# Loading v straight behind k and q in a pooled-attention and gated-feed-forward kernel, with the fourth batch's k and q loaded inside the pooling of the third batch's v

## The chip, the cores and the metric

The kernel runs on one core of one Trainium2 chip. The metric is the device time of one execution in microseconds (us). Several unprofiled executions give a median. One further execution was recorded by the hardware profiler, and every instruction time below comes from that one. In the profile PE is TensorE (PEld its weight load), DVE is VectorE, ACT is ScalarE, POOL is GpSimd, and SP is the engine whose queue issues most of the hardware DMAs.

## What is computed

There are 8 batches (numbered 0 to 7 in the code; "the third batch" is number 2, "the fourth" number 3), 8 heads, 576 positions and a head width of 64. The reference, cut to what matters:

```
k_p, v_p = k, v averaged over groups of 8 positions      # 72 keys and values per head
attn = softmax(q @ k_p.T / 8)                            # 576 x 72 per head
x    = (attn @ v_p) as a matrix of 4608 tokens x 512
h    = x @ w_in                                          # 512 -> 2048
out  = (h * cos(h)) @ w_out                              # 2048 -> 512, float32
```

## The kernel before

The feed-forward part works in nine token tiles of 512, `t` = 0 to 8. A batch is 576 tokens, so tile `t` ends inside batch `t`; its last 64 tokens of batch `t-1` (`REST`) and most of batch `t` make it up. The order of every engine is written out by hand: each engine executes its instructions in program order, and between engines only semaphores hold an instruction back.

Stage `t` of the main loop (L448) first runs the up projection on PE (`up_mm`, L320; 8 pairs of column groups, `fp`), while ACT takes the cosine (L327) and DVE multiplies (L330). It then runs the down projection on PE (`down_mm`, L333; 64 matmuls, counted by `n`). Between these 64 matmuls stand, at places given by the list `fill` (L508), the attention of batch `b = t+1`: scores (L213), exponentials (L220), and `values_rows`, which multiplies with the pooled values (L300), normalises on DVE (L301, L303) and sends the result `x_r` through a DMA transpose on SP's queue into `xT` (L304). There are four such transposes in a stage, a first pair (`n` = 18 and 19) and a second pair (`n` = 42 and 44). `xT` is what the next stage's up projection reads. For stage 2 (tile columns 1024 to 1535) that includes the first three of the four transposed blocks of batch 2; every later stage needs fewer blocks of its newest batch.

The inputs of attention are staged by POOL, and these are what the change touches:

- `load_kv` (L100 to L105) issues a DMA on POOL's own queue that reads k or v of a batch in float32 and leaves bf16. Its tile comes from a pool of two buffers (`kvst`) that k and v take in turn, so v(b) uses the buffer that v(b-1) used, and k(b) that of k(b-1). `load_q` (L107) does the same for q, whose tiles have two buffers of their own.
- `pool_add` (L134) adds up the groups of 8 on POOL: one large add (L141), one half its output's size (L144), then for k two small ones into `kp2` (L147) and for v one into `vz` (L150). Its argument `then` is called after the first add.
- `q_transpose` (L186) and `k_transpose` (L173) are DMA transposes on SP's queue, issued in the up projection of stage `t` after `fp` 0 and `fp` 2. They make `qT` and `kk`, which the scores read.
- The copy into `gate` (L525) is a one-element copy that reads `kk`. It makes POOL wait until the k transpose has landed before it issues the next batch's loads.

At the end of stage `t`'s code stand POOL's steps for batch `b+1`, so POOL's order for it is: gate, load k, load q, first add of k, load v, rest of k, all of v:

```
        if 0 < t and b + 1 < B:

            nc.gpsimd.tensor_copy(out=gate, in_=kk[b % 2][0:1, 0, 0:1])
        if b + 1 < B:
            load_kv(b + 1, "k", k)
            load_q(b + 1)
            pool_add(b + 1, "k", lambda: load_kv(b + 1, "v", v))
            pool_add(b + 1, "v")
```

Batches 0 and 1 are loaded and pooled differently (on PE) and the change leaves them alone.

Of the kernel before, what the change touches and what calls it, by code (L numbers as in the profile page):

```python
# [12 lines left out]
ADD = mybir.AluOpType.add  # L13
# [6 lines left out]
def kernel(  # L20
# [9 lines left out]
    nc = tc.nc  # L30
    B, H, S, D = q.shape
# [35 lines left out]
    kk = [wpool.tile([128, H, SpA], BF16, name=f"kk{i}") for i in range(2)]  # L67
# [10 lines left out]
    staged = {}  # L78
# [4 lines left out]
    def load_even(dst, b, src, j0=0, j1=KCH):  # L83
        nc.gpsimd.dma_start(out=dst[:, j0:j1].rearrange("p j t d -> p j (t d)"), in_=even_view(src, b, j0, j1))  # L84

    def kv_tile():
        return kvst.tile([128, 2 * H * POOL * D], BF16, name="kv_st", tag="kv_st")
# [9 lines left out]
    def q_tile(b):  # L97
        staged["q", b] = qst.tile([128, KCH, ROW, D], BF16, name="q_b", tag="q_b")

    def load_kv(b, which, src):  # L100

        st = kv_tile()[:Sp].rearrange("p (i h t d) -> p i h t d", i=2, h=H, t=POOL)
        nc.gpsimd.dma_start(out=st[:, 0].rearrange("p h t d -> p h (t d)"),
                            in_=src[b].rearrange("h (p t) d -> p h (t d)", t=POOL))
        staged[which, b] = st  # L105

    def load_q(b):  # L107
        q_tile(b)
        load_even(staged["q", b], b, q)
# [15 lines left out]
    def v_part(b):  # L125
        return vz[b % 2][:, :, 0:4:3, :]
# [4 lines left out]
            for r in range(2):  # L131
                copy(out=dst[half[r], pj0:pj1, a, 0:Sp], in_=ps[half[a]])

    def pool_add(b, which, then=None):  # L134

        st = staged.pop((which, b))
        x = st[:, 0]
        s = st[:, 1].rearrange("p h t d -> p (h t d)").bitcast(FP32).rearrange(
            "p (h t d) -> p h t d", h=H, t=POOL // 2)
        add = nc.gpsimd.tensor_tensor  # L140
        add(out=s, in0=x[:, :, 0:4, :], in1=x[:, :, 4:8, :], op=ADD)  # L141
        if then is not None:
            then()
        add(out=s[:, :, 0:2, :], in0=s[:, :, 0:2, :], in1=s[:, :, 2:4, :], op=ADD)  # L144
        if which == "k":
            for slot in range(2):
                add(out=kp2[b % 2][:Sp, :, slot, :], in0=s[:, :, 0, :], in1=s[:, :, 1, :], op=ADD)  # L147
        else:
            s = s.rearrange("p (j a) t d -> p j a t d", a=2)
            add(out=v_part(b), in0=s[..., 0, :], in1=s[..., 1, :], op=ADD)  # L150

    def pool_k_mm(b, bank, pj0, pj1):

        kb = staged["k", b]
        ps = bank[:, 0:(pj1 - pj0) * Sp].rearrange("p (j n) -> p j n", n=Sp)
        for pj in range(pj0, pj1):
            for t in range(ROW):
                for rows in half:
                    nc.tensor.matmul(ps[rows, pj - pj0, :], lhsT=kb[rows, pj, t, :], rhs=groups[rows, t, :],  # L159
                                     start=(t == 0), stop=(t == ROW - 1))  # L160
        return lambda copy: put_kk(b, ps, pj0, pj1, copy)
# [10 lines left out]
    def k_transpose(b):  # L172
        nc.sync.dma_start_transpose(out=kk[b % 2], in_=kp2[b % 2].rearrange("p h s d -> p (h s d)"))  # L173
# [14 lines left out]
    def q_transpose_mm(b, bank, g0, g1):  # L188

        if ("qT", b) not in att:  # L190
            qT_tile(b)
        ps = bank.bitcast(BF16)[:, 0:(g1 - g0) * 128].rearrange("p (g n) -> p g n", n=128)
        for g in range(g0, g1):
            nc.tensor.matmul(ps[:, g - g0, :], q_flat(b)[:, g * 128:(g + 1) * 128], identity, is_transpose=True)  # L194
        return lambda copy: copy(out=att["qT", b][:, g0:g1, :], in_=ps)
# [114 lines left out]
    def sin_tables():  # L310
        nc.scalar.preload_act_table_set("trig_and_small")  # L311


    def up_mm(t, fp, k0=0, k1=KCH):

        h = banks[fp % 3]
        for j in range(2):
            fc = 2 * fp + j
            for ki in range(k0, k1):
                nc.tensor.matmul(h[:, j, :], lhsT=w_in_sb[fc // 4][:, ki, (fc % 4) * 128:(fc % 4 + 1) * 128],  # L320
                                 rhs=xT[:, ki, t * TILE:(t + 1) * TILE],
                                 start=(ki == 0), stop=(ki == KCH - 1))

    def up_g(t, fp, between=()):
        h = banks[fp % 3]
        cos = msb.tile([128, 2, TILE], FP32, name="cos", tag="cos", bufs=2)
        nc.scalar.activation(out=cos, in_=h, func=ACTF.Sin, bias=half_pi[:, :1])  # L327
        for put, copy in between:
            put(copy)
        nc.vector.tensor_mul(out=g_sb[:, 2 * fp:2 * fp + 2, :], in0=h, in1=cos)  # L330
# [38 lines left out]
    for rows in half:  # L369
# [15 lines left out]
                            in1=first_of.unsqueeze(1).to_broadcast([128, ROW, Sp]), op=mybir.AluOpType.subtract)  # L385
# [6 lines left out]
    gate = consts.tile([1, 1], BF16, name="gate")  # L392
# [52 lines left out]
    up_mm(0, 1, 0, 2)  # L445
    sin_tables()

    for t in range(NT):  # L448
        b = t + 1
        if t > 0:  # L450

            up_mm(t, 0, 0, 2)
            up_mm(t, 1, 0, 2)
        for fp in range(FFCH // 2):
            up_mm(t, fp, 2 if fp < 2 else 0)
            between = ()
            if t == 0:
                if fp == 4:
                    puts = pool_k_mm(1, obanks[0], 0, 2), pool_k_mm(1, obanks[1], 2, 4)
                elif fp in (5, 6):  # L460
                    g0 = 9 * (fp - 5)
                    puts = q_transpose_mm(1, obanks[0], g0, g0 + 5), q_transpose_mm(1, obanks[1], g0 + 5, g0 + 9)
                if fp in (4, 5, 6):
                    puts[0](vec)
                    between = ((puts[1], act),)
            up_g(t, fp, between)
            if 0 < t and b < B:
                if fp == 0:
                    q_transpose(b)
                elif fp == 2:  # L470
                    k_transpose(b)
        mms = [(ms, fc) for ms in range(4) for fc in range(FFCH)]
        if t == 0:
            mms = [(ms, fc) for hm in range(2) for cg in range(4) for ms in range(2 * hm, 2 * hm + 2)
                   for fc in range(4 * cg, 4 * cg + 4)]


        def S_(n, bank):
            return lambda: scores(b, us[n], banks[bank])

        later = []

        def V_(n, bank, wait=None):
            return lambda: values(b, us[n], banks[bank], wait)

        fill = []
        if t < B:
            exp_tables()
            fill = [(1, lambda: scores(t, REST, banks[2])), (16, lambda: values(t, REST, banks[1]))]
        if t == 0:  # L490
            fill[1:] = [(2, S_(0, 0)), (8, lambda: pool_v_mm(1, banks[1])), (8, lambda: values(t, REST, banks[2])),
                        (11, S_(1, 0)), (13, V_(0, 1)), (18, S_(2, 2)), (21, V_(1, 0, later)), (26, S_(3, 1)),
                        (32, lambda: later.pop()()), (32, V_(2, 2)), (40, V_(3, 0))]
        elif b < B:
            us = BY_TOKENS

            def scores_of(*parts):

                def go():
                    for f in scores_mm, scores_exp:  # L500
                        for b_, u, bank in parts:
                            f(b_, u, banks[bank])
                return go

            def rows_of(i, blk, bank):
                return lambda: values_rows(b, us[2 * i:2 * i + 2], blk, banks[bank])

            fill = [(4, scores_of((b, us[0], 2), (b, us[1], 0))), (18, rows_of(0, 0, 1)), (19, rows_of(0, 1, 2)),  # L508
                    (29, scores_of((b, us[2], 0), (b, us[3], 1), (t, REST, 2))),
                    (42, rows_of(1, 0, 0)), (44, rows_of(1, 1, 1)), (47, lambda: values(t, REST, banks[2]))]  # L510
        fi = 0
        if t == NT - 1:
            mms = mms[:-FFCH]
        for n, (ms, fc) in enumerate(mms):
            while fi < len(fill) and fill[fi][0] <= n:
                fill[fi][1]()
                fi += 1
            down_mm(obanks[ms % 2], ms, fc)
            if fc == FFCH - 1:
                down_out(t, ms, obanks[ms % 2])  # L520
        if t < B:
            sin_tables()
        if 0 < t and b + 1 < B:

            nc.gpsimd.tensor_copy(out=gate, in_=kk[b % 2][0:1, 0, 0:1])  # L525
        if b + 1 < B:
            load_kv(b + 1, "k", k)
            load_q(b + 1)
            pool_add(b + 1, "k", lambda: load_kv(b + 1, "v", v))
            pool_add(b + 1, "v")  # L530
    last_chunk()
# [1 line left out]
_INS = ['q', 'k', 'v', 'moe_w_in', 'moe_w_out']  # L533
# [26 lines left out]
```

## Time and profile before

| what | value |
|---|---|
| median of 3 unprofiled runs | 300.61 us (299.97 to 300.97) |
| the profiled execution's own time | 303.76 us |
| its span, first to last instruction | 302.0 us |
| mean granted TensorE clock | 0.988 of full |
| PE busy | 287.4 us (95% of the span) |
| DVE, ACT, POOL busy | 158.7, 162.0, 130.6 us |
| packets of POOL's DMA queue (q0) | 18.07 MB, 39.9% of 16 engines' span |
| packets of SP's DMA queue (q1) | 17.57 MB, 31.0% |

The profiled execution is 3.15 us longer than the median, and 1.76 us of its time lies around the span. A timeline line gives start, duration, engine, line of the kernel, operation, output and input, count, and in brackets how long the engine stood idle before it and what released it. A line of waits gives the engine and instruction that waited, what it waited for, the sum in us, how often, and the longest. A line of stretches gives the window, its length, the busy time of each engine with instruction counts, the granted clock as a share of full speed, the mean busy share of the 16 DMA engines (records may overlap, so it can pass 1), and GB/s. A line on a DMA's landing gives the minimum, median and maximum from issue to landing.

### The profile page before, as it was taken

What the parts mean: (1) busy time and instruction counts of PE and PEld (TensorE: products, weight loads), DVE (VectorE), ACT (ScalarE), POOL (GpSimd) and SP (SyncE); (2) the same over time, 40 slices, a digit from 0 to 9 for tenths busy, and PEclk for the clock granted to TensorE, in tenths of its full rate; (3) what the DMA queues carried; (4) which work ended last, traced back from release to release, by engine and by line L of the source; (5) the groups of instructions that cost most, each with busy time, mean ns of one, the idle gap of its engine ahead of it and who ended that gap; (6) DMA issues with size and microseconds to landing.
All of it is one profiled execution on the core that took longest, in us unless ns stands there. A gap on an engine that the chain in (4) does not pass through costs nothing.

```text
span 302.0 us, 4739 instructions
## 1 busy us (share of the span) xinstructions
PE 287.4 (95%) x1878; PEld 140.2 (46%) x1912; DVE 158.7 (53%) x212; ACT 162.0 (54%) x182; POOL 130.6 (43%) x93
## 2 busy tenths in 40 slices
PE   6889999999949999999999999999999999999995
PEld 2545544445514455445544544455445544444444
DVE  6358546574504645564557454745475547425712
ACT  3886897465504655465546554655465646605500
POOL 8463008692958296329492956284900000000000
PEclk9999999999978999999999999999999999999999
DMA  7999996929992976776998597679902430131023
GB/s 148 205 207 207 207 199 130 180 65 131 169 210 42 151 77 145 169 99 91 156 200 119 84 174 160 96 116 142 203 0 54 87 72 0 35 72 35 0 66 75
DMA packets 57221, 36.07 MB, mean 119 GB/s; under 512 B 35184, under 2 KB 52464, under 8 KB 57200
## 3 DMA queue, kind: packets, MB, share of 16 engines
q0 software_dynamic: 19744, 18.07, 39.9%
q1 hardware_dynamic: 37216, 17.57, 31.0%
q8 instruction: 15, 0.25, 0.3%
q10 hardware_dynamic: 240, 0.13, 0.2%
q14 instruction: 6, 0.05, 0.0%
HBM read 36.70 MB, written 9.44 MB: 153 GB/s over the span
## 4 chain that ended last, share of the span: by engine, by line
PE 90%; DMA 6%; issue 1%; POOL 1%; DVE 1%; DVEq 0%; POOLq 0%
PE bank L320 42%; PE obank L333 38%; DMA kv_st<-in_v_dram 3%; PE bank L213 3%; DMA xT<-x_r 3%; PE bank L300 2%; PE bank L243 1%; PE bank L351 1%; PE bank L167 1%; POOL q_b L84 1%; PE obank L159 0%; PE obank L282 0%; PE obank L194 0%; DVE xT L284 0%; DVE vz L169 0%
## 5 line engine op out<-in xcount | busy, mean ns | idle before, releaser
L320 PE MATMUL bank<-xT,w_in_sb 128*128 128x512 bf16 x564 | 128.6, 385 | 4.8 <-DMA xT<-x_r 4.2
L333 PE MATMUL obank<-w_out_sb,g_sb 128*128 128x512 bf16 x540 | 127.8, 379 | 1.3 <-issue 0.6
L327 ACT ACTIVATE cos<-bank,half_pi 128x1024 f32<-128x1024 f32 x72 | 79.2, 1113 | 77.7 <-PE bank L320 77.7
L330 DVE TENSOR_TENSOR g_sb<-bank,cos 128x1024 bf16<-128x1024 f32 x72 | 87.3, 1224 | 58.8 <-ACT cos L327 58.8
L320 PEld LDWEIGHTS <-w_in_sb 128*128 128x128 bf16 x576 | 56.6, 99 | 74.0 <-issue 4.9
L333 PEld LDWEIGHTS <-g_sb 128*128 128x128 bf16 x560 | 51.6, 98 | 56.6 <-issue 1.9
L141 POOL TENSOR_TENSOR kv_st<-kv_st 72x2048 f32<-72x2048 bf16 x12 | 48.7, 4058 | 66.7 <-DMA kv_st<-in_k_dram 46.4
L339 DVE COPY o_sb<-obank 128x512 f32<-128x512 f32 x35 | 24.2, 692 | 46.9 <-PE obank L333 45.6
L220 ACT ACTIVATE ex<-bank 72x1024 bf16<-72x1024 f32 (+1 forms) x40 | 35.0, 928 | 21.0 <-PE bank L213 20.9
L144 POOL TENSOR_TENSOR kv_st<-kv_st 72x1024 f32<-72x1024 f32 x12 | 28.3, 2355 | 0.6
L249 ACT ACTIVATE lnc<-bank 64x256 f32<-64x256 f32 (+1 forms) x24 | 10.8, 449 | 17.9 <-PE bank L243 17.7
L254 DVE TENSOR_TENSOR xT<-bank,inv 64x256 bf16<-64x256 f32 (+1 forms) x24 | 12.3, 511 | 10.8 <-ACT inv L250 10.6
L303 DVE TENSOR_TENSOR x_r<-bank,inv_r 128x512 bf16<-128x512 f32 x24 | 16.6, 692 | 0.8
L147 POOL TENSOR_TENSOR kp<-kv_st 72x512 bf16<-72x512 f32 x12 | 14.9, 1265 | 0.5
L213 PE MATMUL bank<-qT,kk 64*72 64x256 bf16 (+1 forms) x192 | 12.1, 250 | 0.3 <-issue 0.3
L308 ACT ACT_TABLE_LOAD x9 | 11.5, 1283 | 0.9 <-PEq L544 0.7
L213 PEld LDWEIGHTS <-kk 64*72 64x72 bf16 x192 | 7.9, 110 | 8.5 <-issue 7.2
L311 ACT ACT_TABLE_LOAD x9 | 11.5, 1283 | 0.2
L300 PEld LDWEIGHTS <-ex 72*128 72x128 bf16 x192 | 8.9, 97 | 5.0
L301 DVE RECIPROCAL inv_r<-bank 128x8 f32<-128x8 f32 x24 | 4.9, 203 | 10.7 <-PE bank L300 10.7
L300 PE MATMUL bank<-vz,ex 72*128 72x65 bf16 x192 | 9.8, 193 | 0.1
L84 POOL DMA_DIRECT2D q_b<-in_q_dram x10 | 7.8, 784 | 2.2 <-DMA w_in_sb<-in_moe_w_in_dram 1.4
(59 smaller groups left out, 105.1 us busy)
## 6 DMA issues: line engine op xcount, KB each, us to landing
out_dram<-o_sb SPq DMA_DIRECT2D x70, 128.0 KB, 2.9
kv_st<-in_v_dram POOLq DMA_DIRECT2D x8, 576.0 KB, 9.4
kv_st<-in_k_dram POOLq DMA_DIRECT2D x7, 576.0 KB, 7.6
q_b<-in_q_dram POOLq DMA_DIRECT2D x6, 576.0 KB, 9.6
w_in_sb<-in_moe_w_in_dram POOLq DMA_DIRECT2D x4, 512.0 KB, 13.8
w_out_sb<-in_moe_w_out_dram POOLq DMA_DIRECT2D x4, 512.0 KB, 18.2
q_b<-in_q_dram POOLq DMA_DIRECT2D x4, 288.0 KB, 12.6
g_sb<-in_k_dram SPq DMA_DIRECT2D x1, 576.0 KB, 3.6
```

The lines of the kernel that those rows point to most:

```text
L141: add(out=s, in0=x[:, :, 0:4, :], in1=x[:, :, 4:8, :], op=ADD)
L144: add(out=s[:, :, 0:2, :], in0=s[:, :, 0:2, :], in1=s[:, :, 2:4, :], op=ADD)
L147: add(out=kp2[b % 2][:Sp, :, slot, :], in0=s[:, :, 0, :], in1=s[:, :, 1, :], op=ADD)
L213: nc.tensor.matmul(pair[:Sp, bank, c:c + n].rearrange("p (g n) -> p g n", n=64), lhsT=kk[b % 2][half[r], h0 + i, 0:Sp], rhs=att["qT", b][h ...
L220: nc.scalar.activation(out=ex[:, 0:nh * n].rearrange("p (a n) -> p a n", a=2), in_=pair[:Sp, :, 0:nh * n // 2], func=ACTF.Exp, scale=scale ...
L300: nc.tensor.matmul(out[:, pj, hp * (D + 1):(hp + 1) * (D + 1)], lhsT=ex[:, c:c + 128], rhs=v1)
L303: nc.vector.tensor_mul(out=x, in0=vals, in1=inv.unsqueeze(3).to_broadcast([128, KCH, 2, D]))
L320: nc.tensor.matmul(h[:, j, :], lhsT=w_in_sb[fc // 4][:, ki, (fc % 4) * 128:(fc % 4 + 1) * 128], rhs=xT[:, ki, t * TILE:(t + 1) * TILE], st ...
L327: nc.scalar.activation(out=cos, in_=h, func=ACTF.Sin, bias=half_pi[:, :1])
L330: nc.vector.tensor_mul(out=g_sb[:, 2 * fp:2 * fp + 2, :], in0=h, in1=cos)
L333: nc.tensor.matmul(o, lhsT=g_sb[:, fc, ms * 128:(ms + 1) * 128], rhs=w_out_sb[fc // 4][:, fc % 4, :], start=(fc == 0), stop=(fc == FFCH - 1))
L339: nc.vector.tensor_copy(out=o[:, 0:n], in_=ps)
```

## The change

`pool_add` no longer calls a function between its adds. It can be run whole, or as its first add alone (`part` 0), or as all but its first add (`part` 1). The gate and the loads of k and q are put into a function `load_next`.

- In all stages the load of v is issued directly behind the load of q, before POOL's first add of k. It used to stand behind that add.
- At the end of stage 0 only the first add of v of batch 2 is issued. Its other adds come in stage 1, after `k_transpose(2)`, behind the gate and the loads of k and q of batch 3; the load of v of batch 3 follows them.
- At the end of stage 1 only the pooling adds of batch 3 are left, since its loads have been issued already.

```
@@ -131,16 +131,17 @@
-    def pool_add(b, which, then=None):
-
-        st = staged.pop((which, b))
+    def pool_add(b, which, part=None):
+
+        st = staged[which, b]
...
-        add(out=s, in0=x[:, :, 0:4, :], in1=x[:, :, 4:8, :], op=ADD)
-        if then is not None:
-            then()
+        if part != 1:
+            add(out=s, in0=x[:, :, 0:4, :], in1=x[:, :, 4:8, :], op=ADD)
+        if part == 0:
+            return
...
@@ -445,6 +446,13 @@
+    def load_next(b):
+
+        if b > 1:
+            nc.gpsimd.tensor_copy(out=gate, in_=kk[b % 2][0:1, 0, 0:1])
+        load_kv(b + 1, "k", k)
+        load_q(b + 1)
+
@@ -469,6 +477,10 @@
                 elif fp == 2:
                     k_transpose(b)
+                    if t == 1:
+                        load_next(b)
+                        pool_add(b, "v", 1)
+                        load_kv(b + 1, "v", v)
@@ -520,14 +532,12 @@
-        if 0 < t and b + 1 < B:
-
-            nc.gpsimd.tensor_copy(out=gate, in_=kk[b % 2][0:1, 0, 0:1])
         if b + 1 < B:
-            load_kv(b + 1, "k", k)
-            load_q(b + 1)
-            pool_add(b + 1, "k", lambda: load_kv(b + 1, "v", v))
-            pool_add(b + 1, "v")
+            if t != 1:
+                load_next(b)
+                load_kv(b + 1, "v", v)
+            pool_add(b + 1, "k")
+            pool_add(b + 1, "v", 0 if t == 0 else None)
```

The orders of PE, DVE, ACT and SP are the same in both kernels, instruction for instruction. POOL has the same instructions in another order.

## The prediction

> **What bounds the kernel now.** I read the span in 40 slices first. PE is at 9 tenths almost everywhere, and its clock leaves full speed in one place, slices 12 and 13 (83 to 98 us). Next came the waits, which name one large wait of PE.
>
> ```profile
> PE   6889999999949999999999999999999999999995
> PEclk9999999999978999999999999999999999999999
> ```
>
> ```profile
> PE bank L320 <- DMA xT<-x_r: 4.2, 1, 4.2
> POOL gate L525 <- DMA kk<-kp: 8.2, 2, 4.8
> ```
>
> PE's timeline puts the wait between stages 1 and 2: PE ends the down projection at 83.74 and the up projection starts at 87.94, when a transpose of x_r has landed. The chain of waits shows the same DMA on the path for 8.31 us. The stages in stretches price it:
>
> ```profile
> 79.91 3.83 PE L333 MATMUL obank<-w_out_sb,g_sb 128*128 128x512 bf16 x16
> 87.94 16.63 PE L320 MATMUL bank<-xT,w_in_sb 128*128 128x512 bf16 x63 [4.19 <-DMA xT<-x_r]
> ```
>
> ```profile
> 53.40:87.94 34.54, 30.04 (x189) 14.40 (x191) 17.41 (x23) 16.88 (x18) 22.17 (x15) 0.98 0.96 139
> 87.94:120.91 32.97, 32.80 (x189) 15.24 (x193) 16.02 (x21) 16.89 (x18) 23.81 (x13) 0.92 0.71 121
> 120.91:151.27 30.36, 30.15 (x190) 14.55 (x193) 16.71 (x22) 16.88 (x18) 15.01 (x11) 1.00 0.87 131
> 151.27:181.60 30.33, 29.91 (x189) 14.54 (x192) 16.71 (x22) 16.88 (x18) 21.23 (x12) 1.00 0.88 142
> ```
>
> Stages 3 to 6 take 30.30 to 30.40 us, PE bound. Stage 1 is longer by its wait, 4.19 us; stage 2 takes 32.97, that is 2.62 us over the mean 30.35, at a mean clock of 0.92. The wait so costs 4.19 + 2.62 = 6.81 us. Elsewhere after the start PE waits for nothing long, so this is all that POOL's order can give back.
>
> Why the transpose is late is read from landings. SP issues the second pair of stage 1 at 79.6 and 80.9, just behind v's load, which POOL issued at 78.78. It lands after 7.4 and 8.3 us. In stage 2 the second pair is issued at 116.9, v's load (from 107.48) having landed at 115.8, and it lands after 2.4 us.
>
> ```profile
> L304 SPq DMA_TRANSPOSE xT<-x_r x2: 1192/1258/1325, 79.6 to 80.9; - x2
> DMA to landing us min/median/max: 7.4/7.9/8.3
> ...
> L304 SPq DMA_TRANSPOSE xT<-x_r x2: 1191/1208/1226, 116.9 to 118.2; - x2
> DMA to landing us min/median/max: 2.4/2.4/2.4
> ```
>
> POOL's timeline gives the steps that move:
>
> ```profile
> 59.18 4.07 POOL L141 TENSOR_TENSOR kv_st<-kv_st 72x2048 f32<-72x2048 bf16 x1 [2.89 <-DMA kv_st<-in_v_dram]
> 63.33 2.35 POOL L144 TENSOR_TENSOR kv_st<-kv_st 72x1024 f32<-72x1024 f32 x1
> 65.76 1.27 POOL L150 TENSOR_TENSOR vz<-kv_st 72x512 bf16<-72x512 f32 x1
> 66.98 0.18 POOL L525 COPY gate<-kk 1x1 bf16<-1x1 bf16 x1
> 67.10 0.86 POOL L103 DMA_DIRECT2D kv_st<-in_k_dram  x1
> 67.96 0.79 POOL L84 DMA_DIRECT2D q_b<-in_q_dram  x1
> 74.76 4.06 POOL L141 TENSOR_TENSOR kv_st<-kv_st 72x2048 f32<-72x2048 bf16 x1 [6.02 <-DMA kv_st<-in_k_dram]
> 78.78 0.86 POOL L103 DMA_DIRECT2D kv_st<-in_v_dram  x1
> ```
>
> **Stage 0: v of batch 2 ahead of the first add of k.** The issue (0.87) waits for its buffer, which PE stops reading at 37.66 (pooling of batch 1's v). POOL stands idle until 46.45 for k of batch 2, so wait and issue cost nothing; k and q were issued before, and in the same queue v follows them. q landed at 28.46 + 20.7 = 49.2. v then lands by 49.2 + 8.6 = 57.8 at most (8.6 is its whole time to landing before), and by about 54 if only a load's spacing is added (k and q of one batch land 2.8 to 3.5 us apart). k's later adds start 0.87 us earlier, so k is pooled at 55.4, and v's first add runs from there, or at the latest from 57.8: it ends between 59.5 and 61.9. I take 59.5.
>
> **Stage 1: the gate and k, q of batch 3 inside v's pooling.** The gate now waits for `kk` of batch 2; queued behind it are two load issues, v's last adds, and so `vz`, which PE reads at 71.63. In this execution that k transpose was issued at 60.36 and landed 2.8 us later, 63.2. The q transpose ahead of it on SP took 4.36 us to issue beside v's load; without such a load it took 2.0 to 2.2 (stages 3, 4), so I take 58.2 for the k transpose and 61.0 for the gate; ends 61.0 and 63.2. Then k 0.86, q 0.79, adds 2.35 and 1.27, with the gaps of the listing some 5.5 us: `vz` ready at 66.5 (at most 68.7, before it was 67.03), 3 to 5 us ahead of PE. v of batch 3 is issued at 66.5, not 78.78.
>
> Its landing: at most 10.2 us (the longest v load in the rows, beside a pair of transposes) after issue, 76.7; or counted by loads, q lands 11 us after k's issue (67.10 to 78.2), 72.1, and v one load (half of the 9.4 that two need beyond 1.6 of start) later, 76.8. From the late gate 79.0. So v is in by 76.8, ahead of the second pair at 79.6. It now runs beside the first pair (73.3 and 74.7), which before ran beside q and landed after 6.1 and 7.0 us. I take those times again, 81.8 at the latest; the row for a pair that wholly runs beside v, stage 3, has 8.6 and 9.6 us, which would be 84.4. The first of the second pair, the one that PE waited for, then lands at 79.6 + 2.4 = 82.0. PE wants it at 83.74. The wait of 4.19 us goes, and with it the low clock. What is late next is the end of PE's own down projection, with about 1.7 us to spare. DVE's last write to xT ends at 82.2.
>
> The Trainium skill (TensorE: Matmul & The Clock Gate, Part 1) says an idle window of about 3.4 us halves the clock; here it was at half from 86.5 to 93.3, 2.8 us after PE stopped. By that rule any leftover wait well under 3 us would cost itself alone.
>
> A rule of the Trainium skill speaks against the change: the page DMA: Bandwidth & Descriptors (Queues, rings and completion order) has each engine take turns between queues packet by packet. My estimate by that rule is about twice 2.4 us for a pair beside v; it would land at 84.4, PE would wait 0.7 us, and there would be no more than that to win. The 7.4 to 8.3 us measured here decide against it.
>
> **Stages 2 to 6: v directly behind q.** POOL issues the same DMA one place earlier (0.86 us in an idle of 5.5 to 6.3 us for k), so k's first add is not delayed. v lands some 15 to 16 us after k's issue, not 21 to 22. In stage 3 k was issued at 128.6; v would land near 144 instead of 150.4. The first pair there is issued at 141.0 and 142.3 and landed after 8.6 to 9.6 us, near 150.8, just before the stage's end at 151.27; with v in at 144 it lands earlier. Cost 0; the cover is POOL's idle time, and without it 0.86 us per stage would fall on POOL, which has slack to the gate. I gain nothing here either, as PE waits for no DMA in these stages.
>
> **Sum.** Profiled execution: 303.76 - 4.19 - 2.62 = 296.95 us, span 295.2. The median lies 3.15 us below the profiled time. PE's stages repeat to 0.1 us, so a DMA wait is what can differ between executions, and I read the unprofiled ones as losing about 3.65 us (300.61 - 296.95) at the same place. Then they too end near 296.9. If instead recording costs all 3.15 us, 6.81 comes off 300.61: 293.8. I take 296.9, nearer the row that repeats.
>
> **Rivals.** (1) Part of the wait stays: the three loads run on into the second pair. For: three loads and a pair share 16 engines. Against: 3 us between 76.8 and 79.6. Stage 3's second pair, issued as v ended, took 4.1 to 4.8 us, which lands at 84.4 and leaves 0.7 us, 297.6; a wait of 3 us without the low clock gives 299.95.
>
> (2) The change does not do what it says: the pair was slow for its own queue (four outputs, q and k transposes follow) and not for v. Then nothing moves, 300.6. Against: the 2.4 us of stage 2 with the same SP order.
>
> (3) Slower: the gate, now in front of v's last adds, holds `vz` back. It decides when `kk` lands after 71.63 - 5.5 = 66.1; each us beyond is a us of PE wait, and from about 2.8 us another 2.6 for the clock. To end 0.9 us over the median it must land at about 69: 296.95 + 2.9 + 2.6 = 302.4. For: gate waits of 4.8 us occur. Against: in stage 1 it landed at 63.2 even beside v.
>
> **Chances.** 0.3% (0.9 us) is about what measurement tells from no change. All of the wait gone 0.72; rival 1 0.12, most of it below 299.7; rival 2 0.06; rival 3 0.10. Faster 0.72 + 0.11 = 0.83; same 0.06 + 0.01 = 0.07; slower 0.10. The range goes from 293.8 to 299.7, leaving out rivals 2 and 3 and the end of rival 1, 0.17.
>
> **What would show it.** Right: no wait of PE L320 for xT<-x_r, clock at full throughout stage 2, stages 1 and 2 both near 30.35 us; v of batch 3 issued near 66.5, gate at about 61; second pair of stage 1 landing after 2.4 us. Wrong: a PE wait at L300 in stage 1 (`vz`), or the second pair still landing after 5 us or more with v already in, or a second place that loses time where the unprofiled runs lost it.

## The result and the profile after

The changed kernel takes 296.43 us (median of 4, 296.36 to 296.98). The kernel before took 300.79 us beside it (median of 4, 299.97 to 301.95). The ratio is 0.9856, 95% interval 0.9821 to 0.9891. The profiled execution takes 296.36 us with a span of 294.6, against 303.76 and 302.0 before. The profiled execution of the kernel before was one of its slow ones, so the gain is the 4.36 us between the medians and not the 7.4 us between the profiles.

The span in 40 slices of the changed kernel has no dent in PE and no fall of its clock (line numbers are one higher than before from L141 to L446, the copy into `gate` is now L452, and the experiments shift some lines further):

```profile
PE   8899999999999999999999999999999999999995
PEclk9999999999999999999999999999999999999999
```

Its PE timeline at the end of stage 1 goes from the down projection to the up projection with no idle time in brackets. The windows of stages 1, 2 and 3 are all 30.35 or 30.36 us long, with the clock at 1.00.

```profile
79.48 3.83 PE L334 MATMUL obank<-w_out_sb,g_sb 128*128 128x512 bf16 x17
83.16 14.01 PE L321 MATMUL bank<-xT,w_in_sb 128*128 128x512 bf16 x64
```

```profile
52.80:83.16 30.36, 30.36 (x194) 14.56 (x193) 16.73 (x23) 16.89 (x18) 26.02 (x15) 1.00 0.85 138
83.16:113.51 30.35, 30.35 (x194) 14.59 (x193) 16.71 (x22) 16.89 (x18) 20.86 (x12) 1.00 0.78 136
113.51:143.86 30.35, 30.35 (x193) 14.59 (x192) 16.70 (x22) 16.89 (x18) 18.59 (x12) 1.00 0.79 136
```

The landings of stage 1's second pair of transposes, and POOL's steps that lead to it, in the changed kernel:

```profile
L305 SPq DMA_TRANSPOSE xT<-x_r x2: 1190/1214/1237, 79.1 to 80.4; - x2
DMA to landing us min/median/max: 2.5/2.5/2.5
```

```profile
61.65 0.18 POOL L452 COPY gate<-kk 1x1 bf16<-1x1 bf16 x1 [2.28 <-DMA kk<-kp]
62.23 0.86 POOL L103 DMA_DIRECT2D kv_st<-in_k_dram  x1 [0.40 <-POOL gate L452]
66.33 1.27 POOL L151 TENSOR_TENSOR vz<-kv_st 72x512 bf16<-72x512 f32 x1
67.89 0.86 POOL L103 DMA_DIRECT2D kv_st<-in_v_dram  x1 [0.30 <-POOL vz L151]
```

The landing of v of batch 3, in the kernel before and then in the changed kernel:

```profile
L103 POOL DMA_DIRECT2D kv_st<-in_v_dram x1: 861/861/861, 78.8 to 78.8; - x1
DMA to landing us min/median/max: 8.9/8.9/8.9
```

```profile
L103 POOL DMA_DIRECT2D kv_st<-in_v_dram x1: 861/861/861, 67.9 to 67.9; - x1
DMA to landing us min/median/max: 9.0/9.0/9.0
```

Before, v landed at 78.78 + 8.9 = 87.7 and the first of the pair at 79.58 + 8.3 = 87.9. Now v is issued at 67.89 and lands 9.0 us later, at 76.9. That is 2.2 us before the pair is issued. The first of the pair lands at 79.15 + 2.5 = 81.65, 1.5 us before PE wants it.

Of the 7.4 us between the spans, 4.19 is the wait and 2.62 the slow stage 2. About 0.4 of the rest is there before stage 1 begins (PE's up projection starts at 52.80 against 53.23). That start lies between 52.47 and 53.77 in the 13 profiles of this case, so the 0.4 is within what executions differ by.

### The profile page after: what moved, and what is told of

Its sections match the earlier page's. It is cut to its first block, busy times and chain, and to the rows that moved or that the text cites. A ratio compares the mean times of both kernels' runs of the same rounds, so it can differ in the third digit from the quotient of the medians.

```text
span 294.6 us, 4775 instructions
## 1 busy us (share of the span) xinstructions
PE 287.7 (98%) x1912; PEld 140.2 (48%) x1912; DVE 158.8 (54%) x212; ACT 162.1 (55%) x182; POOL 130.5 (44%) x93
## 4 chain that ended last, share of the span: by engine, by line
PE 93%; DVE 1%; issue 0%; DVEq 0%
PE bank L321 42%; PE obank L334 42%; PE bank L214 3%; PE bank L301 2%; PE bank L244 1%; PE bank L352 1%; PE obank L160 0%; PE bank L168 0%; PE obank L283 0%; PE obank L195 0%; DVE xT L285 0%; DVE vz L170 0%; DVE o_sb L340 0%; DVEq L285 0%
## 5 line engine op out<-in xcount | busy, mean ns | idle before, releaser
L334 PE MATMUL obank<-w_out_sb,g_sb 128*128 128x512 bf16 x560 | 131.4, 379 | 0.0
L321 PE MATMUL bank<-xT,w_in_sb 128*128 128x512 bf16 x576 | 126.6, 379 | 0.0
L321 PEld LDWEIGHTS <-w_in_sb 128*128 128x128 bf16 x576 | 56.1, 98 | 67.6 <-issue 1.6
L452 POOL COPY gate<-kk 1x1 bf16<-1x1 bf16 x5 | 0.9, 180 | 22.7 <-DMA kk<-kp 22.7
L302 DVE RECIPROCAL inv_r<-bank 128x8 f32<-128x8 f32 x24 | 4.8, 202 | 10.7 <-PE bank L301 10.7
```

Of the source, the lines that this page charges most:

```text
L334: nc.tensor.matmul(o, lhsT=g_sb[:, fc, ms * 128:(ms + 1) * 128], rhs=w_out_sb[fc // 4][:, fc % 4, :], start=(fc == 0), stop=(fc == FFCH - 1))
```

## The experiments

**One part at a time.** The first kernel has only v straight behind q, in all stages. Against the changed kernel:

```
-                    if t == 1:
-                        load_next(b)
-                        pool_add(b, "v", 1)
-                        load_kv(b + 1, "v", v)
...
-            if t != 1:
-                load_next(b)
-                load_kv(b + 1, "v", v)
+            load_next(b)
+            load_kv(b + 1, "v", v)
             pool_add(b + 1, "k")
-            pool_add(b + 1, "v", 0 if t == 0 else None)
+            pool_add(b + 1, "v")
```

> The first part alone: in every stage v is issued straight behind q, and nothing of the fourth batch moves inside the pooling of the third batch's v. Theory (what costs time is v of batch 3 in flight beside the second pair of x_r transposes of stage 1): POOL pools v of batch 2 by about 63.1, passes the gate at 63.2, issues k, q, v of batch 3 at 63.4, 64.2, 65.0; v lands about 14.5 us after k's issue, 78, before the pair is issued at 79.2. No PE wait, full clock, 296.4 us, the same as the changed kernel. Rival (both parts are needed, since only the earlier k and q free the engines in time): a wait of PE for xT of 1 to 4 us stays, 297.5 to 301.

Measured: 296.50 us, ratio to the kernel before 0.9855 (0.9815 to 0.9896). PE does not wait for xT. v of batch 3 is issued at 64.86 and lands at 79.9, later than the 78 expected and 0.7 us after the pair's issue at 79.12; the pair still lands after 2.5 to 2.8 us. The first part alone gives the whole gain: the changed kernel's 296.43 us shows nothing that the second part adds to it.

The second kernel has only stage 1's new order. Against the changed kernel, with a `then` added to `pool_add` as it was before:

```
             if t != 1:
                 load_next(b)
-                load_kv(b + 1, "v", v)
-            pool_add(b + 1, "k")
+            pool_add(b + 1, "k", None, None if t == 1 else lambda: load_kv(b + 1, "v", v))
```

> The second part alone: v stays behind the first add of k in every stage but 1; in stage 1 k and q of batch 3 are issued inside the pooling of v of batch 2 and v of batch 3 behind that pooling. Theory: v of batch 2 lands near 59, its first add ends near 63.2, k of batch 3 is issued at 63.4, v of batch 3 near 69, landing near 78.5, just before the second pair at 79.2: no or nearly no PE wait, 296.4 to 296.9 us. Rival (both parts are needed): v of batch 3 lands after 80, a wait of 1 us or more, 297.5 to 301.

Measured: 297.24 us, ratio 0.9877 (0.9836 to 0.9918). v of batch 3 lands at 68.79 + 9.6 = 78.4 and the wait at the end of stage 1 is gone. So either part is enough for that wait. A small wait appears one stage later, at the end of stage 2, in this kernel's PE timeline:

```profile
114.51 5.80 PE L323 MATMUL bank<-xT,w_in_sb 128*128 128x512 bf16 x26 [0.67 <-DMA xT<-x_r]
```

There v of batch 4, still behind the first add of k, was issued at 102.19 and landed at 112.7, after the second pair's issue at 109.7; the first of that pair landed at 114.4.

**Moving the load of v of batch 3 alone.** Two kernels leave everything else of the change in place. In the first this load goes behind k's first add:

```
                     if t == 1:
                         load_next(b)
                         pool_add(b, "v", 1)
-                        load_kv(b + 1, "v", v)
...
-            pool_add(b + 1, "k")
+            pool_add(b + 1, "k", None, (lambda: load_kv(b + 1, "v", v)) if t == 1 else None)
```

> The changed kernel with only the load of v of batch 3 put back behind the first add of k of batch 3: issued near 73.8 and not at 67.9, landing near 83. Theory: the second pair (issued 79.2) lands with it, at 83 to 84; PE wants it at 83.2: a wait of 0 to 1 us, too short for the clock, 296.4 to 297.4 us. Rival (the pair was slow for its own queue, not for v): the pair lands after 2.5 us, no wait, 296.4.

In the second it goes behind all adds of k:

```
-                        load_kv(b + 1, "v", v)
...
             pool_add(b + 1, "k")
+            if t == 1:
+                load_kv(b + 1, "v", v)
```

> The changed kernel with only the load of v of batch 3 put back behind all adds of k of batch 3: issued near 78.7, where the kernel before issued it. Theory: the second pair lands with it at about 87.5, PE waits 4.2 us and the clock falls to half again: span 301 to 302, time 300 to 303.5 us, as the kernel before. Rival (the pair was slow for its own queue, or the gain came from the other moved steps): 296.4 to 297.

Measured: 297.35 us (0.9877, 0.9823 to 0.9931) and 301.60 us (1.0034, 1.0009 to 1.0059). Issued at 74.66, v lands at 83.4, the first of the pair at 84.7, and PE waits 0.43 us:

```profile
84.72 14.02 PE L323 MATMUL bank<-xT,w_in_sb 128*128 128x512 bf16 x64 [0.43 <-DMA xT<-x_r]
```

Issued at 78.26, v lands at 86.1, the first of the pair at 86.6, PE waits 3.49 us, and the clock falls; stage 2 takes 31.88 us. These are PE's line, the pair's landing and the windows of stages 1 and 2 of the second kernel:

```profile
86.62 13.61 PE L321 MATMUL bank<-xT,w_in_sb 128*128 128x512 bf16 x55 [3.49 <-DMA xT<-x_r]
```

```profile
L305 SPq DMA_TRANSPOSE xT<-x_r x2: 1189/1278/1367, 79.0 to 80.2; - x2
DMA to landing us min/median/max: 6.7/7.2/7.6
```

```profile
52.60:86.62 34.02, 30.53 (x194) 14.48 (x192) 17.44 (x24) 16.89 (x18) 22.57 (x15) 1.00 0.83 127
86.62:118.50 31.88, 31.88 (x192) 15.00 (x193) 16.01 (x21) 16.90 (x18) 26.22 (x14) 0.95 0.67 126
```

One load, put back to where it stood, takes back the whole gain. The gain comes from when v of batch 3 is in flight.

**Fewer bytes of the same load.** In the kernel before, `load_kv` and `pool_add` handle 4 heads and not 8 for v of batch 3:

```
+        nh = H // 2 if which == "v" and b == 3 else H
...
+        x, s = x[:, 0:nh], s[:, 0:nh]
```

> The kernel before, but of v of batch 3 only 4 of 8 heads are loaded and pooled (the others keep an older batch's values). Theory (the second pair lands when v has landed): issued at 78.8 as before, half of v lands near 84, the pair with it, PE waits 0 to 1 us, the clock stays full: 296.4 to 297.8 us. Rival (transposes beside any load are slow by a fixed amount, or v's bytes do not matter): the wait of 3 to 4 us and the low clock stay, 299.5 to 302.

Measured: 297.10 us (0.9875, 0.9812 to 0.9938). Half of v is issued at 79.52 and lands at 85.2. The first of the pair, issued at 79.5, lands at 85.6; PE waits 1.95 us and the clock stays full:

```profile
L104 POOL DMA_DIRECT2D kv_st<-in_v_dram x1: 750/750/750, 79.5 to 79.5; - x1
DMA to landing us min/median/max: 5.7/5.7/5.7
```

```profile
L307 SPq DMA_TRANSPOSE xT<-x_r x2: 1217/1272/1326, 79.5 to 80.9; - x2
DMA to landing us min/median/max: 4.9/5.5/6.1
```

```profile
85.58 14.02 PE L323 MATMUL bank<-xT,w_in_sb 128*128 128x512 bf16 x63 [1.95 <-DMA xT<-x_r]
```

The wait is longer than the 0 to 1 us expected, since half of v landed 1.2 us later than the 84 expected: POOL issued it 0.7 us later than in the profile of before, and it took 5.7 us, not 5.2. The profiled execution, 298.79 us, was also the longest of the four. The pair still lands just behind v. A delay of the same length beside any load does not fit this: the first of the pair took 6.1 us, and 8.3 beside the whole of v.

**How early is early enough.** Two kernels move one load of v each, in the kernel before. The first puts only v of batch 3 straight behind its q, the second only v of batch 2:

```
+            if t == 1:
+                load_kv(b + 1, "v", v)
-            pool_add(b + 1, "k", lambda: load_kv(b + 1, "v", v))
+            pool_add(b + 1, "k", None if t == 1 else lambda: load_kv(b + 1, "v", v))
```

> The kernel before with only the load of v of batch 3 moved, straight behind q of batch 3 (v of batch 2 and all later stages as before). Theory: k of batch 3 is issued at 67.1, v at 68.8 and not 78.8, landing near 82; the second pair (79.6) lands at 82.5 to 83.5, before PE wants it at 83.7 or just behind. Then the wait goes to the end of stage 2, where v of batch 4, still behind the first add of k, lands near the second pair: 0 to 1 us there. 296.5 to 297.8 us. Rival (v of batch 2 has to come earlier too): v of batch 3 lands after 83.5, a wait of over 1 us in stage 1, 298 or more.

> The kernel before with only the load of v of batch 2 moved, straight behind q of batch 2. Theory (what counts is when POOL passes the gate of stage 1): POOL passes it near 63.2 and not 67.0; v of batch 3, still behind the first add of k, is issued near 74.7 and not 78.8 and lands near 83.4; the second pair (79.2) lands near 84, PE waits 0.4 to 1 us, too short for the clock: 296.8 to 298 us. Rival (v of batch 3 itself has to be moved): a wait of 2 us or more in stage 1, 299 or more.

The second has `t == 0` in these lines. Measured: 301.26 us (0.9984, 0.9944 to 1.0025) and 300.10 us (0.9937, 0.9895 to 0.9979). Both expectations were missed, in the direction of their rivals. In the first kernel k, q and v of batch 3 go out at 65.93, 66.78, 67.56, and v lands 15.9 us after its issue, at 83.5; the first of the pair lands at 85.0. PE waits 1.90 us in the profiled execution. That one took 298.29 us and was the shortest of ten; the others took up to 302.19, and the six above 301 show a mean granted clock of 0.988 to 0.994, the other four 0.998 or more. So the profile does not show the typical wait of this kernel.

```profile
85.11 14.02 PE L320 MATMUL bank<-xT,w_in_sb 128*128 128x512 bf16 x63 [1.90 <-DMA xT<-x_r]
```

In the second, v of batch 3 is issued at 75.66 and lands 10.3 us later, and PE waits 2.95 us; executions took 297.04 to 301.90.

```profile
86.73 3.63 PE L320 MATMUL bank<-xT,w_in_sb 128*128 128x512 bf16 x16 [2.95 <-DMA xT<-x_r]
```

Each move alone brings v forward by some 2 to 4 us and ends inside the collision. Both together (with the same order in stages 2 to 6, the first experiment) bring it out, and so does the second part of the change.

**Stages 2 to 6.** The changed kernel with v behind k's first add in these stages, and the changed kernel once more beside it:

```
             if t != 1:
                 load_next(b)
+            if t == 0:
                 load_kv(b + 1, "v", v)
-            pool_add(b + 1, "k")
+            pool_add(b + 1, "k", None, (lambda: load_kv(b + 1, "v", v)) if t > 1 else None)
```

> The changed kernel once more, beside the next two: 296.4 to 297 us, no PE wait for xT in any stage.

> The changed kernel with the load of v put back behind the first add of k in stages 2 to 6 (stages 0 and 1 as changed). By the prediction these stages gain nothing: 296.4 to 297, the same as the changed kernel. By what the kernel with the second part alone showed (a PE wait of 0.67 us at the end of stage 2): v of batch 4 is issued near 102.1, lands near 112.5, the second pair of stage 2 with or behind it near 114, PE waits 0.5 to 0.8 us there: 297.0 to 297.4.

Measured: 296.32 us (0.9821, 0.9790 to 0.9852) and 296.57 us (0.9827, 0.9799 to 0.9856). PE waits for xT in neither. In the second, v of batch 4 was issued at 102.79 and landed after 8.7 us, at 111.5; stage 2's second pair, issued at 109.6, landed after at most 3.3 us. The 0.67 us wait of the kernel with the second part alone, where the same load took 10.5 us, did not return. These stages give no gain that shows here, and only little room is left at the end of stage 2.

**What the clock adds.** The kernel before, with 12 matmuls of a constant tile inside PE's wait:

```
         if t > 0:
+            if t == 2:
+                warm_up(12, banks[0][:, 0, :])
             up_mm(t, 0, 0, 2)
```

> The kernel before with 12 matmuls of the constant tile (2.6 us of PE) ahead of stage 2's up projection, inside PE's wait. Theory (the wait costs its own length, and once more for the clock that falls to half): the wait left is shorter by 2.6 us, the up projection starts when it did, but the clock stays full and stage 2 takes about 30.4 us from there. About 296.4 + 3.5 to 4.2 = 299.9 to 300.6 us, 0.5 to 2.6 us below the kernel before of the same call. Rival (the low clock costs nothing by itself): the time of the kernel before.

In the profile the mechanism is as expected: 0.64 us of wait are left behind the 12 matmuls, the clock stays at 1.00, and stage 2 takes 30.36 us. The windows of the filled wait and of stage 2:

```profile
83.61:87.00 3.39, 2.75 (x13) 1.08 (x12) 0.69 (x1) 0.00 (x0) 0.55 (x2) 1.00 1.15 165
87.00:117.36 30.36, 30.04 (x188) 14.58 (x193) 16.02 (x21) 16.89 (x18) 20.86 (x12) 1.00 0.79 131
```

The time is not settled: median 300.12 us against 301.14, but the ratio's interval is 0.9954 to 1.0044. The kernel before alone ran from 298.38 to 304.20 beside it. The gap that the 12 matmuls stood in was 3.39 us in this profile, so that the clock would have fallen without them is likely from the other profiles and not shown by this one.

**The rival that was to be slower.** The changed kernel, with 8.2 us of repeated adds on POOL behind the gate of stage 1:

```
         if b > 1:
             nc.gpsimd.tensor_copy(out=gate, in_=kk[b % 2][0:1, 0, 0:1])
+        if b == 2:
+            for _ in range(2):
+                pool_add(b, "v", 0)
         load_kv(b + 1, "k", k)
```

> The changed kernel with the first add of v of batch 2 done twice more (8.1 us, the same values) between the gate and the loads of stage 1: what a gate that opens 8 us late would do. Theory: vz is ready at about 75.7 and not 67.6; PE wants it at 71.2, waits about 4.5 us, and the clock falls: 296.4 + 4.5 + 2.6 = 303.5 us, slower than the kernel before; without the clock 300.9. v of batch 3 is then issued at 76 and lands near 86, but the second pair moves with PE to about 86, so no second wait. Rival (the loads being late matter more than vz): a second PE wait for xT behind the first, over 305.

Measured: 302.59 us, ratio 1.0040 (1.0010 to 1.0069). `vz` is ready at 74.7, PE waits for it, and no wait for xT follows. Stage 1 takes 35.70 us with a mean clock of 0.95: 3.54 of wait and 1.8 of low clock over 30.35.

```profile
74.76 0.59 PE L301 MATMUL bank<-vz,ex 72*128 72x65 bf16 x8 [3.54 <-POOL vz L151]
```

The mechanism exists and makes the kernel slower, but it needs the gate to open over 3.6 us late (`vz` is ready at 67.6 in the changed kernel, PE wants it at 71.2).

## Why the prediction was right

- **Where the time was.** The wait between stages 1 and 2 and its low clock went in full; stages 1 and 2 are now 30.36 and 30.35 us (30.35 was taken). The predicted span was 295.2, the measured one 294.6, the predicted time 296.9 and the measured one 296.43. The difference is mostly the 0.4 us ahead of stage 1, which no step of the change accounts for and which is within what that start varies by.
- **Stage 0.** v of batch 2 landed at 37.52 + 16.7 = 54.2 ("about 54" was taken, 57.8 at most), under k's adds, which ended at 55.3. The 54 does not follow from the spacing given for it, 2.8 to 3.5 us, which makes it 52.0 to 52.7; v landed 5.3 us behind q.
- **Gate and vz.** Without v's load beside it the q transpose took 2.16 us to issue (2.0 to 2.2 was taken), the k transpose went out at 58.79 (58.2), the gate opened at 61.65 (61.0), and `vz` was ready at 67.6 (66.5). The sum left out two semaphore gaps on POOL, 0.40 and 0.30 us, behind the gate and behind `vz`.
- **Landing of v of batch 3.** 76.9 against 76.8. That it agrees to 0.1 us is luck, since two errors cancel: it was issued 1.4 us later than taken and landed 9.0 and not 10.2 us after issue. The first pair, beside it, landed after 5.5 and 6.4 us, near the 6.1 and 7.0 taken.
- **Second pair.** 2.5 us against 2.4, landing at 81.65 against 82.0.
- **Stages 2 to 6.** The load cost nothing and gained nothing measurable, as predicted. In stage 3 v now lands 14.5 us after k's issue (15 to 16 was taken), and the first pair after 4.1 to 5.0 us in place of 8.6 to 9.6.
- **Profiled time and median.** The prediction read the 3.15 us between them as a wait that differs between executions, not as a cost of recording. The changed kernel supports this: its profiled executions, 296.36 and 296.02, are no longer than its others. The kernel before ran from 297.88 to 305.82 beside the experiments. The granted clock of each of these 55 executions agrees with a wait that differs: the 11 up to 300.17 us kept 0.998 or more, and of the 44 from 300.68 us on all but one show 0.983 to 0.994. The waits themselves are only seen in profiles.
- **Rivals.** That the pair was slow for its own queue fell with the load moved alone (3.49 us of wait back) and with half the bytes. The late gate is real, but far. Part of the wait remaining (rival 1) is what the half moves got; in the changed kernel v clears the pair's issue by 2.2 us, and in the first experiment there was no wait with v landing 0.7 us after that issue. One row against rival 1 was misread: stage 3's second pair was not issued as v ended but at 147.3, 3 us before v landed at 150.4, so its 4.1 to 4.8 us say nothing of a pair behind a load.
- **One size was off.** The low clock was priced at 2.6 us from a wait of 2.8 us on. A wait of 2.95 us left the clock full, 3.49 and 3.54 us cost 1.5 and 1.8, and only 4.19 cost 2.62. In the kernel with the late gate the wait was 3.54 and not 4.5 and the term 1.8 and not 2.6, which makes 301.8 from 296.4; its profiled execution took 301.54, its median is 302.59, and 303.5 was written down.
- **The rule on turns between queues.** The prediction's estimate by this rule (the Trainium skill, DMA: Bandwidth & Descriptors, Queues, rings and completion order) left 0.7 us to win. The runs went against that estimate: the first of the pair landed 0.2 to 1.6 us after the load in all seven profiles with a wait for `xT` at the end of stage 1 (before, v of batch 3 behind the first add, behind all adds, half of v, v of batch 3 alone, v of batch 2 alone, the 12 matmuls). The packet records of the kernel before show it directly: from 82.2 to 84.0 us POOL's queue finished 244 packets (250 KB) and SP's queue none, though nine of its packets were under way.

## What to carry to other kernels

When a transfer that somebody waits for is slow, look for the bulk load beside it, and price the wait by when that load lands; in this kernel that was right, and a share of the engines was not. A load that is moved and still lands behind the transfer's issue may pay or not: here four such kernels took 0.9855, 0.9877, 0.9937 and 0.9984 of the time before. The load's own spread (7.5 to 10.7 us from issue to landing for v behind the first add of k, in all profiles) is about as large as what these moves brought forward. Add to a wait of an engine with a granted clock what the clock takes afterwards.

## What the runs showed of the hardware

- Transposes on SP's queue hardly advanced while a load on POOL's queue was moving: a pair took 2.4 to 2.5 us from issue to landing where v had landed before, 7.4 to 8.3 beside v of batch 3, and with half of v 6.1 us for the first of the pair, 0.4 us after that load. In the kernel before, six of SP's packets of 256 bytes that began between 82.0 and 82.2 us took 3.3 to 3.6 us each. Why they stood is not shown. Not every slow transpose had a load beside it: with v behind all adds of k, one issued at 74.0 us took 4.3 us while POOL's queue moved nothing.
- The low clock came in spells of 3.4 or 6.8 us: one of 6.8 with the wait of 4.19 us (86.5 to 93.3), one of 3.4 with 3.49 (86.3 to 89.8) and with 3.54 (74.8 to 78.2), none with 2.95 or 1.95. They began 2.8, 3.2 and 3.6 us after PE's last matmul, so the length of the wait alone did not decide: 2.8 us was enough once, and 2.95 was not. The Trainium skill (TensorE: Matmul & The Clock Gate, Part 1) gives 3.4 us as the length of its free-running window, and the spells agree with one and two of it.
- A load of v issued behind k and q on the same queue, ahead of the first add of k, landed more nearly by when k went out than by its own issue: for batch 3, 14.0 to 17.5 us after k's issue in six profiles, while its own issue-to-landing time ran from 8.3 to 15.9 us.
